# A new fixed order of work in an attention + SiLU kernel: one chain of loads, denominators in four steps, other spacing of idle matmuls

## Chip, cores, metric

One core of a Trainium2 chip. The metric is device microseconds of one execution. A run is marked slow when it is over 1.5% above the fastest of the same kernel; ratios are taken from fast runs alone. Every comparison below is with runs of the kernel before on the same chip.

## The reference

Polynomial-sketch attention (4 batches, 4 heads, 1088 rows, head size 32, sketch size 8), whose output feeds a feed-forward layer with SiLU:

```python
def phi(x):                                    # 8 x 8 products of two sketches
    a = np.einsum('rd,bhsd->bhsr', S1, x)
    b = np.einsum('rd,bhsd->bhsr', S2, x)
    return np.einsum('bhsi,bhsj->bhsij', a, b).reshape(*x.shape[:-1], r * r)
q_p, k_p = (phi(q), phi(k))
kv  = np.einsum('bhsf,bhsd->bhfd', k_p, v)
z   = np.sum(k_p, axis=2)
num = np.einsum('bhsf,bhfd->bhsd', q_p, kv)
den = np.einsum('bhsf,bhf->bhs', q_p, z)[..., None] + 1e-06
x   = (num / den).transpose(0, 2, 1, 3).reshape(4352, 128)
h   = x @ w_in                                 # 128 -> 2048
out = (h / (1 + np.exp(-h))) @ w_out           # 2048 -> 128
```

## The kernel before

The kernel first lists all its work as tasks: an engine (or a choice of two), a cost in us, what it needs. A long constant, ORDER, then says in which order the tasks are issued and, where there is a choice, on which engine. A small model replays that order to choose buffers, and to decide how many idle matmuls to put in front of each TensorE task before the second layer starts. An idle matmul multiplies zeros and nobody reads its result; it is there to keep TensorE busy, so that its clock rises sooner.

```python
ORDER = """
0 7 74 28 23 1 29 24 2.1 22 33 4 3.0 30 25 32 8 34 97 31 35 42.1 11 5 140 40.0 37 6 36 102 55 50 16
...                                            # cut: number of a task, ".1" picks the second engine
"""

def emit(self, text, handles, fill, until):    # in class Plan
    seq = self.order(text)
    self.replay(seq)                           # modelled start and end of each task
    last = 0.0
    for t, c in seq:
        if t["on"] == "PE":
            if last < until():
                fill(last, min(t["start"], until()))
            last = t["end"]
        ...                                    # cut: calls the task's function

def fill(lo, hi):                              # until(): the modelled start of the first h
    step = 0.213 if lo < 4.6 else 0.11
    for _ in range(max(0, int((hi - max(lo, 0.9) - 0.02) / step))):
        nc.tensor.matmul(hold["bank"][:, 0:256], zero[:, 0:P], zero, start=True, stop=True)

def scale():                                   # denominators of a whole batch: one task on VectorE
    nc.vector.tensor_tensor(out=aw[:, :, 0:R], in0=grp(0), in1=grp(2), op=ALU.mult)
    nc.vector.tensor_reduce(out=st["den"], in_=aw, axis=AX.X, op=ALU.add)
    nc.vector.reciprocal(out=st["den"], in_=st["den"])
    nc.vector.tensor_tensor(out=st["aqs"], in0=grp(0), in1=_bc(st["den"], 1, R), op=ALU.mult)

def dmat(i):                                   # qp -> qt by a transposing DMA, on SP's queue
    nc.sync.dma_start_transpose(st["qt", i], st["qp", i].rearrange("p g i j -> p (g i j)"))
```

Names in the profile: PE is TensorE, DVE VectorE, ACT ScalarE, POOL GpSimd, and SP the engine whose queue (SPq) issues most of the DMAs. Kx, Qx, Vf are loaded inputs; KT, QT their 32 x 32 transposes (VectorE); kab and qabm the sketches; kp and qp the products of sketches; KV, kvx, KVd the key-value sums; xT the attention output; H the 2-buffer TensorE result of the first matmul, G its SiLU (ScalarE); ot the final output.

## Time and profile before

| | kernel before |
|---|---|
| time, median of 3 runs | 99.42 us (98.66 to 99.92) |
| span of the profiled run | 97.2 us |
| first SiLU starts | 17.61 |
| batch 1: its keys' first transpose on VectorE | 15.39 |
| batch 1: its first SiLU (number 17 of 68) | 39.32 |
| from there to the end | 57.9 |

These are starts, in us from the span's start. Two rows of the page before, in 40 slices of 2.4 us, matter later: TensorE's busy tenths and the clock that was granted to it.

```profile
PE   5999979969999769999999999999499999999910
PEclk9999999999999999999999999999999999999997
```

The single 4 (near 68 us) is batch 3's numerator, for which TensorE waits. The clock row shows full speed from the start, though the matmuls of the first 10 us run at half rate: this row does not show the warm-up.

### The profile page before, as it was taken

How to read it: one execution, taken by the hardware profiler on the slowest of the kernel's cores; microseconds unless marked ns; L12 is line 12 of the kernel's file. 1: busy time of each engine (PE TensorE's matmuls, PEld its weight loads, DVE VectorE, ACT ScalarE, POOL GpSimd, SP SyncE). 2: the span in 40 equal slices, each digit the busy share in tenths (PEclk: the TensorE clock that was granted, in tenths of full speed). 3: DMA queues.
4: the chain of work that ended last, by engine and by line, in shares of the span. 5: the costliest groups of instructions: out<-in, count | busy, mean ns of one | idle time of the engine just before them, and what ended most of it. 6: DMA issues, size and time to landing. Idle time of an engine off the chain costs nothing.

```text
span 97.2 us, 2474 instructions
## 1 busy us (share of the span) xinstructions
PE 86.4 (89%) x961; PEld 51.4 (53%) x970; DVE 56.7 (58%) x148; ACT 74.0 (76%) x95; POOL 38.3 (39%) x48
## 2 busy tenths in 40 slices
PE   5999979969999769999999999999499999999910
PEld 4545548746677434444533444444244477879900
DVE  5676589999899999999744962804132220022210
ACT  3321546958899929899998799999589999999810
POOL 5048705199998980089920059900000000000000
PEclk9999999999999999999999999999999999999997
DMA  1998999978952573336960000968210336004420
GB/s 34 262 304 226 321 414 402 346 230 253 328 231 61 104 140 59 84 88 133 182 126 4 0 0 8 166 99 152 44 27 0 59 49 108 7 22 85 75 76 14
DMA packets 28506, 12.93 MB, mean 133 GB/s; under 512 B 23120, under 2 KB 26704, under 8 KB 28496
## 3 DMA queue, kind: packets, MB, share of 16 engines
q1 hardware_dynamic: 28256, 12.72, 50.3%
q8 instruction: 7, 0.11, 0.5%
q10 hardware_dynamic: 240, 0.07, 0.3%
q14 instruction: 3, 0.02, 0.1%
HBM read 8.79 MB, written 2.23 MB: 113 GB/s over the span
## 4 chain that ended last, share of the span: by engine, by line
PE 72%; DVE 13%; DMA 5%; SPq 3%; issue 2%; DVEq 0%
PE H L726 25%; PE B L743 21%; PE B L869 7%; PE B L740 6%; DMA qt<-qp 5%; DVE KT L304 3%; SPq L698 3%; PE H L618 2%; PE H L272 2%; PE B L272 2%; DVE qp L646 2%; PE B L333 1%; DVE QT L610 1%; PE B L658 1%; DVE ot L748 1%
## 5 line engine op out<-in xcount | busy, mean ns | idle before, releaser
L730 ACT ACTIVATE G<-H 128x1024 bf16<-128x1024 f32 x68 | 64.8, 1034 | 6.0 <-PE H L726 5.4
L726 PE MATMUL H<-xT,w_in 128*128 128x512 bf16 (+1 forms) x157 | 37.5, 336 | 0.0
L743 PE MATMUL B<-G,w_out 128*128 128x512 bf16 (+1 forms) x122 | 30.9, 351 | 0.6 <-issue 0.3
L726 PEld LDWEIGHTS <-w_in 128*128 128x128 bf16 x176 | 18.4, 114 | 10.8 <-issue 2.2
L327 POOL TENSOR_TENSOR kp<-kab 128x512 bf16<-128x512 f32 (+1 forms) x18 | 17.9, 1014 | 1.9 <-DVE kab L321 1.9
L743 PEld LDWEIGHTS <-w_out 128*128 128x128 bf16 x128 | 12.1, 98 | 10.3 <-issue 0.9
L646 POOL TENSOR_TENSOR qp<-aqs,qabm 128x1024 bf16<-128x1024 f32 (+1 forms) x5 | 10.1, 2019 | 13.7 <-DVE aqs L641 13.7
L869 PE MATMUL B<-zero 128*128 128x256 bf16 x52 | 10.5, 353 | 1.1 <-DVE fmask L233 1.1
L304 DVE STREAM_TRANSPOSE KT<-Kx 128x576 f32<-128x576 f32 (+4 forms) x10 | 9.1, 955 | 0.9 <-DMA Kx<-in_k_dram 0.9
L748 DVE STREAM_TRANSPOSE ot<-B 128x512 f32<-128x512 f32 (+1 forms) x8 | 5.1, 642 | 7.1 <-PE B L743 6.9
L869 PEld LDWEIGHTS <-zero 128*128 128x128 bf16 x52 | 5.9, 122 | 3.6 <-DVE fmask L233 1.0
L164 DVE COPY ot<-B 128x128 f32<-128x128 f32 x5 | 1.3, 287 | 10.3 <-PE B L740 10.3
L478 POOL TENSOR_TENSOR qp<-aqs,qabm 128x512 bf16<-128x512 f32 (+1 forms) x4 | 4.8, 1203 | 6.1 <-DVE aqs L473 6.1
L740 PE MATMUL B<-w_out,G 128*128 128x128 bf16 x96 | 6.7, 219 | 0.0
L740 PEld LDWEIGHTS <-G 128*128 128x128 bf16 x96 | 6.0, 98 | 0.8
L164 DVE CAST xT<-B 128x512 bf16<-128x512 f32 (+1 forms) x6 | 3.7, 636 | 3.7 <-PE B L658 3.7
L646 DVE TENSOR_TENSOR qp<-aqs,qabm 128x1024 bf16<-128x1024 f32 (+1 forms) x4 | 4.4, 1126 | 0.0
L610 DVE STREAM_TRANSPOSE QT<-Qx 128x1024 f32<-128x1024 f32 x3 | 3.6, 1210 | 0.0
L630 DVE STREAM_TRANSPOSE qabm<-H 128x256 f32<-128x256 f32 x6 | 2.5, 417 | 1.9 <-PE B L618 1.9
L618 PE MATMUL H<-QT,WQ 32*32 32x288 f32 x48 | 2.3, 412 | 1.3 <-DVE QT L612 1.3
L499 PE MATMUL B<-identb,qp 128*128 128x128 bf16 x18 | 1.8, 220 | 1.7 <-DVE kab L321 0.9
L327 DVE TENSOR_TENSOR kp<-kab 128x512 bf16<-128x512 f32 x3 | 2.9, 976 | 0.0
(103 smaller groups left out, 78.2 us busy)
## 6 DMA issues: line engine op xcount, KB each, us to landing
Kx<-in_k_dram SPq DMA_DIRECT2D x3, 544.0 KB, 7.0
Qx<-in_q_dram SPq DMA_DIRECT2D x3, 544.0 KB, 6.4
out_dram<-ot SPq DMA_DIRECT2D x24, 64.0 KB, 2.0
Vf<-in_v_dram SPq DMA_DIRECT2D x8, 144.0 KB, 4.1
Vf<-in_v_dram SPq DMA_DIRECT2D x8, 128.0 KB, 3.2
w_inf<-in_moe_w_in_dram SPq DMA_DIRECT2D x2, 512.0 KB, 7.1
w_outf<-in_moe_w_out_dram SPq DMA_DIRECT2D x4, 256.0 KB, 9.4
out_dram<-ot SPq DMA_DIRECT2D x18, 32.0 KB, 1.6
```

The source lines that it names most:

```text
L164: eng.tensor_copy(out=out, in_=in_)
L304: nc.vector.transpose(out=dst, in_=src.rearrange("p c a d -> p c (a d)"))
L327: eng.tensor_tensor(out=st["kp"][:, H * lo: H * hi], in0=_bc(a, 2, R), in1=_bc(bb, 1, R), op=ALU.mult)
L478: eng.tensor_tensor(out=st[f"qp{lo}"], in0=_bc(st["aqs"][:, H * lo: H * hi], 2, R), in1=_bc(bq.rearrange("p a (h r) -> p (a h) r", h=H), 1 ...
L610: nc.vector.transpose(out=QT[:, :, 0: 32 * NB].rearrange("p c (a s) -> p a c s", s=32), in_=Qx[b][:, 0: 4 * NB, :].rearrange("p (a c) d -> ...
L646: eng.tensor_tensor(out=st["qp", i], in0=_bc(st["aqs"][:, g0: g0 + n], 2, R), in1=_bc(grp(1)[:, g0: g0 + n], 1, R), op=ALU.mult)
L726: nc.tensor.matmul(view(sl, i), w_inj[:, (J * jp + i) // 4, (J * jp + i) % 4, :], x, start=True, stop=True)
L730: nc.scalar.activation(out=sl, in_=cc[jp], func=ACT.Silu)
L740: nc.tensor.matmul(d[:, 0:P], view(cc["g", jp], i)[:, P * t: P * (t + 1)], w_out[:, j, :], start=(j == 0), stop=(j == NJ - 1))
L743: nc.tensor.matmul(cc["o"][:, :n], w_out[:, j, :], view(cc["g", jp], i), start=(j == 0), stop=(j == NJ - 1))
L748: nc.vector.transpose(out=cc["ot"][:, :n], in_=cc["o"][:, :n])
L869: nc.tensor.matmul(hold["bank"][:, 0:256], zero[:, 0:P], zero, start=True, stop=True)
```

## The change

Its intent: start the second layer sooner and close the waits inside it. The order was searched again (with noise on the modelled durations), the loads were tied into one chain so that the search could not permute them, each denominator became four tasks so that other work can stand between them, and the idle matmuls got another spacing in the model. The diff, cut:

```diff
 ORDER = """
-0 7 74 28 23 1 29 24 2.1 22 33 4 3.0 30 25 32 8 34 97 31 35 42.1 11 5 140 40.0 37 6 36 102 55 50 16
+0 7 22 28 23 1 29 24 2.1 25 33 3.0 30 80 32 8 34 106 31 35 38.1 11 5 40.0 36 14 37 6 55 16 50 111
 ...                                           # the whole list is new
-    def scaled(b, aq, mq, lo, hi):            # four instructions, one task (scale() likewise)
+    def scale_tasks(b, aq, mq, g0, n, deps, nm):
+        ...
+        for name, cost, fn, tt in (("prod", 0.07 + 0.0084 * n, prod, True), ("red", 0.07 + 0.0095 * n, red, False),
+                                   ("rec", 0.09 + 0.0078 * n, rec, False), ("norm", 0.07 + 0.0084 * n, norm, True)):
+            deps = [pl.add("DVE", cost, fn, deps, lag=0.1, tt=tt, name=nm(name))]
+        return deps[0]
...
-            c = dma(60 * n, dmat, [o], issue=1.3 if n > 1 else 1.2, lag=1.9, name=nm("dmat"))
+            c = dma(60 * n, dmat, [o], issue=1.3 if n > 1 else 1.2, lag=2.1, name=nm("dmat"))
...
+    loads = ["lqa"] + [f"lv0{c}" for c in range(4)] + ["lqb", "lwi0", "lk1", "lwi1", "lwo0", "lwo1", "lq1", "lwo2", "lwo3"]
+    for b in range(1, B):
+        loads += [f"lk{b}"] * (b > 1) + [f"lv{b}{c}" for c in range(4)] + [f"lq{b}"] * (b > 1)
+    for n0, n1 in zip(loads, loads[1:]):
+        named[n1]["deps"].append(named[n0])
...
     def fill(lo, hi):
-        step = 0.213 if lo < 4.6 else 0.11
+        step = 0.213 if lo < 7.0 else 0.15
```

The instructions of the work itself stay the same in kind and number; 52 idle matmuls become 36.

## The prediction

> **What bounds the kernel now.** I read, in this order, the page's busy times and slices, the costliest groups, ACT's timeline, the chain of work, PE's waits, and SP's timeline.
>
> ```profile
> PE 86.4 (89%) x961; PEld 51.4 (53%) x970; DVE 56.7 (58%) x148; ACT 74.0 (76%) x95; POOL 38.3 (39%) x48
> L730 ACT ACTIVATE G<-H 128x1024 bf16<-128x1024 f32 x68 | 64.8, 1034 | 6.0 <-PE H L726 5.4
> L726 PE MATMUL H<-xT,w_in 128*128 128x512 bf16 (+1 forms) x157 | 37.5, 336 | 0.0
> L743 PE MATMUL B<-G,w_out 128*128 128x512 bf16 (+1 forms) x122 | 30.9, 351 | 0.6 <-issue 0.3
> L869 PE MATMUL B<-zero 128*128 128x256 bf16 x52 | 10.5, 353 | 1.1 <-DVE fmask L233 1.1
> ```
>
> The second layer is 68 units: one PE step into H (L726), one SiLU on ACT (L730), one PE step out (L743 or L740). No SiLU can run before a head has made the first attention output. 52 idle matmuls (L869) fill that head.
>
> ```profile
> 17.61 2.85 ACT L730 ACTIVATE G<-H 128x1024 bf16<-128x1024 f32 x3
> 21.58 1.02 ACT L730 ACTIVATE G<-H 128x1024 bf16<-128x1024 f32 x1 [1.13 <-PE H L726]
> 39.32 1.02 ACT L730 ACTIVATE G<-H 128x1024 bf16<-128x1024 f32 x1 [0.25 <-PE H L726]
> 70.60 1.94 ACT L730 ACTIVATE G<-H 128x1024 bf16<-128x1024 f32 x2 [1.27 <-PE H L726]
> 72.70 12.19 ACT L730 ACTIVATE G<-H 128x1024 bf16<-128x1024 f32 x13 [0.16 <-PE H L726]
> 89.12 2.86 ACT L730 ACTIVATE G<-H 128x1024 bf16<-128x1024 f32 x3 [0.24 <-PE H L726]
> ```
>
> The first SiLU starts at 17.61, the last ends at 91.98, and 5.2 us of last products, copies and stores follow. At full pace a SiLU costs (12.19 - 1.03) / 12 = 0.93 us, so 68 need 63.5 us plus about 2 us of other ACT work; 74.4 us passed. PE's floor is higher: steps in steady state start 0.435 us apart (chain pieces of 0.43), so 68 x 2 x 0.435 = 59.2 us. Attention of batches 1 to 3 and the rest of batch 0 adds, from chain and timeline pieces: three each of key projection 0.72, key sum 0.31, its product 0.18, KV 0.44, query projection 0.78 and numerator 0.34, together 8.3, and transposes and small products 2.5. Floor 70 us; from PE's first step at 16.91 to its last at 92.66, 75.7 us passed. So the time is **head, 70 us of PE, PE's stalls (5.7 us), tail**.
>
> ```profile
> 7.40 0.61 PE H L272 x16
> 8.01 0.40 PE B L802
> 8.42 1.28 PE B L869 x6
> 9.70 0.46 PE B L333 x18
> 10.16 0.33 PE B L869
> ```
>
> This is the chain in the head. The key sum (L333) needs DVE's transposes, done at 8.63, but starts at 9.70: six idle matmuls stand in front. An earlier chain piece has eight of them in 1.82 us ahead of the L272 above, whose input was ready at 6.45.
>
> ```profile
> PE B L658 <- DMA qt<-qp: 1.4, 1, 1.4
> PE H L618 <- DVE QT L612: 1.3, 1, 1.3
> PE B L499 <- DVE kab L321: 0.9, 1, 0.9
> 60.95 3.07 SPq L698 DMA_DIRECT2D out_dram<-ot  x6
> 64.56 1.37 SPq L652 DMA_TRANSPOSE qt<-qp  x1
> ```
>
> PE's stalls: batch 3's numerator waits 1.4 us for a transpose that POOL had fed by 61.26 but SP issued at 64.56, behind six stores; batch 2's query projection waits 1.3 us for DVE.
>
> **What the Trainium skill says.** "TensorE: Matmul & The Clock Gate", Part 1: PE runs at half its 2.4 GHz until a window of about 3.4 us has been busy. The trace agrees on the rate: 1.28 / 6 = 213 ns is 256 columns at 1.2 GHz, and the four idle matmuls at 12.25 start 110 ns apart. It does not agree on the time: pieces turn fast only near 10.2 us, after nine busy us. Same page, "Architectural detail": matmuls run strictly in order, VectorE and ScalarE are strict FIFO. The trace agrees: during the 1.4 us wait on L658, ACT ran dry for 1.27. "SBUF — State Buffer", "SBUF: two separate sides": VectorE with two SBUF inputs and GpSimd lock each other out. The trace agrees: a 1024-column qp on DVE takes 1.22 us at 41.59, and two take 2.79 beside a POOL qp at 30.18. "DMA: Bandwidth & Descriptors", "Issuing engines are not separate DMA queues": transfers interleave. The trace agrees: the w_in loads took 5.8 and 8.3 us, with other loads in flight.
>
> **The change, part by part.**
>
> *Idle matmuls.* The static orders show 36 in place of 52. Between the key projections four stand where eight stood; before the key sum two where six stood. I rework the head with the durations above. Second key projection: PE is free at 5.58 + 4 x 0.23 = 6.5, DVE's KT ends at 6.45, start 6.6 (was 7.40). L802 ends at 7.6, two idle ones at 8.05, the transposes at 7.85: key sum at 8.05 (was 9.70). Then zt, query projection, L349 and WM follow as before, slower by some tenths because PE may be cold: the projection with WM at about 10.4 (was 11.96), the first denominator product at 11.1 (was 12.79). Its four steps take 1.1 us, here with one transpose and one other product between (0.35): the first qp at 12.45 (was 13.88). From that start the old path took 3.73 us to the first SiLU (17.61), and nearly the same pieces stand on it. **Head: -1.4 us.**
>
> *Separate denominator steps.* The four instructions per group remain (0.23 to 0.49 us each on DVE); nothing is saved in work. Others now go between: about neutral, and for batches 0 and 2 it lets a transpose that PE waits for go first.
>
> *Order of work for batch 1.* In the old order DVE does batch 2's key transposes (L304, 1.05 + 0.96) and a second qp of batch 1 (1.4) ahead of things that PE needs. Now the key transposes come after batch 1's first qp, and the second goes to POOL beside it. By hand, DVE's queue gives: batch 0's last group 18.7, batch 1's query transpose 21.4, its projection back by 24.6, denominators 26.8, qp 28.2, POOL's qp 29.5, second transpose issued by 31, numerator at 34.8. The old numerator stood at 37.03. But DVE now has a wait of its own: kvx and KVd of batch 1 come only behind batch 2's key and query transposes, at about 34.1, and the copy of xT behind another 1.05. I get the first SiLU of batch 1 at about 37.0 (was 39.32): **2.3 us ahead, so 0.9 beyond the head**; the PE order has done two more output steps by then (+0.9) and one query projection less (-0.8), which cancel.
>
> *Stores and loads.* Batch 3's three transposes now stand together on SP with no store between, and its two large qp run on DVE and POOL at once (old: 4.25 us in a row on POOL). By the same count they are issued by 60 and land by 64; PE reaches that numerator behind SiLU 49, at about 67. **-1.4 us** if it holds. Loading k2 after w_out and q1 takes one load out of the crowd at 7 to 20 us; the old head shows only 0.84 us of ACT waiting on it, off the chain: 0.
>
> *Given back.* Each query projection takes one of the two H buffers until DVE has emptied it (the old trace shows a 1.01 us ACT gap at 53.98), and that remains. At 16 to 18 us PE meets a key projection whose DVE input I place at 17.4, 0.9 us after PE is ready: already in my 37.0. Later misfits of a new order: +0.6, my guess.
>
> Sum: -1.4 - 0.9 - 1.4 + 0.6 = -3.1. PE's floor checks it: from about 15.5, 70 us and 3.6 of stalls end at 89.1; plus 4.5 of tail is a span of 93.6, -3.6. I take -3.6 to -3.7 and add it to the median: 99.4 - 3.7 = **95.7 us**.
>
> **The rivals.** *Cold clock.* 16 fewer idle matmuls leave PE less busy, so the doubling could come one window (3.4 us) later, near 13.6, or PE could fall back before the first SiLU. For it: the old kernel needed nine dense us. Against: the pieces removed were cold ones in front of real work. It would cost 0.2 to 0.3 us on each of some four pieces on the path and 0.4 per early step: 97 to 98 us.
> *A new DVE wait eats the gain.* kvx of batch 1 sits behind 3 us of transposes; if keys of batch 2 or 3 land late, that grows and PE's in-order queue stops. For: it is the worst wait in my count, and DVE is dense from 21 to 48. Against: loads come earlier. Near 97.5.
> *PE is full anyway.* Slices from 72 on show 9, so an earlier attention may only pile up output steps. That leaves head and numerator: 96.5 to 97.
> *Upside.* If the order also removes the H-buffer gap and the 0.15 to 0.25 us gaps, 93.5.
>
> **Range and chances.** The head gain is the firmest (one visible queue); the other two lean on a count by hand with perhaps 1.5 us of error. I predict 95.7, range 93.4 to 98.0. The limit for faster is 97.4, about one error above my centre: faster 0.80, same 0.17, slower 0.03.
>
> **What would show it.** Right: 36 idle matmuls, none between the end of DVE's kab and the key sum for more than 0.3 us; first SiLU at 15.9 to 16.5; first SiLU of batch 1 at 36 to 38; no DMA wait at the numerator of batch 3; ACT gaps over 0.5 us summing to under 4; tail 5 us as before. Wrong: idle matmuls at 213 ns beyond 11 us, or first steps of 256 columns 0.21 us apart (cold); a wait of PE on kvx or QT over 2 us around 31 to 37; transposes still landing after PE asks.

## The result

The changed kernel took **96.29 us** (median of 4 runs, 95.87 to 96.43) beside 99.19 us of the kernel before (4 runs, 98.66 to 99.92). The ratio of the fast runs is **0.9696**, 95% interval 0.9623 to 0.9769. A ratio here is the mean time of one kernel's fast runs over the mean of the other's in the same rounds, so it is not quite the ratio of the quoted medians.

The page after, the lines that answer to those in the prediction (busy us, share of the span, count):

```profile
PE 84.7 (90%) x943; PEld 48.7 (52%) x954; DVE 57.2 (61%) x151; ACT 73.1 (78%) x92; POOL 37.0 (39%) x48
L733 ACT ACTIVATE G<-H 128x1024 bf16<-128x1024 f32 x68 | 64.5, 1043 | 6.3 <-PE H L729 5.2
L879 PE MATMUL B<-zero 128*128 128x256 bf16 x36 | 8.0, 355 | 1.1 <-DVE fmask L234 1.1
```

The SiLU work is what it was (64.5 us); ScalarE's idle time in front of it has even grown by 0.3 us. The span shrank because the same row of SiLUs starts sooner and its largest late gap is gone. ScalarE's timeline after (start, length, line, group, count, idle before):

```profile
16.45 1.94 ACT L733 ACTIVATE G<-H 128x1024 bf16<-128x1024 f32 x2
37.78 1.02 ACT L733 ACTIVATE G<-H 128x1024 bf16<-128x1024 f32 x1 [0.98 <-PE H L729]
39.54 8.61 ACT L733 ACTIVATE G<-H 128x1024 bf16<-128x1024 f32 x9 [0.74 <-PE H L729]
54.75 6.72 ACT L733 ACTIVATE G<-H 128x1024 bf16<-128x1024 f32 x7 [1.01 <-PE H L729]
61.68 12.17 ACT L733 ACTIVATE G<-H 128x1024 bf16<-128x1024 f32 x13 [0.20 <-PE H L729]
```

The first SiLU starts at 16.45 (before: 17.61), the first of batch 1 at 37.78 (39.32). SiLU 49, which began at 72.70 before, is the tenth of the last group: 61.68 + 9 x 0.93 = 70.05. There is no gap of 1.3 us near it any more. The gap of 1.01 at the query projection of batch 2 is still there.

Why the late gap went, in SP's timeline after: four transposes, batch 3's three among them, stand together ahead of the stores.

```profile
58.84 6.19 SPq L655 DMA_TRANSPOSE qt<-qp  x4
65.13 12.00 SPq L701 DMA_DIRECT2D out_dram<-ot  x12
```

And what TensorE waits for now (total, times, longest, in us), four of the list's six lines; the other two are 1.1 us before the first idle matmul and 0.3 us of "issue". No DMA is in the list:

```profile
PE B L273 <- DVE KT L305: 1.4, 2, 0.8
PE B L513 <- DVE qp L495: 1.2, 2, 0.8
PE B L513 <- POOL qp L495: 0.7, 1, 0.7
PE B L394 <- DVE kvx L165: 0.3, 1, 0.3
```

Two of these lie later: 0.5 us of the first line at 31.6, for batch 2's keys, and the wait on kvx. The rest is in the head or just behind it. The chain of work that ended last shows what is new: it now runs through the load of batch 1's keys and then along VectorE's queue.

```profile
7.15 7.59 DMA Kx<-in_k_dram
14.76 1.10 DVE KT L305
16.74 1.12 DVE KT L305
17.97 0.60 DVE aqs L485
18.60 0.99 DVE qp L495
```

The 7.59 us from issue to landing were off the chain before. A head that is done sooner meets a load that is not.

**The span in parts.** With "k1" for the start of batch 1's key transposes and "17" for the first SiLU of batch 1:

| profiled run | first SiLU | k1 | 17 | span | k1 to 17 | 17 to end |
|---|---|---|---|---|---|---|
| before | 17.61 | 15.39 | 39.32 | 97.2 | 23.9 | 57.9 |
| after | 16.45 | 14.76 | 37.78 | 94.2 | 23.0 | 56.4 |

0.6 us come from an earlier k1, 0.9 from a shorter way to batch 1's first SiLU, 1.5 from what follows: 3.0 us together, the difference of the spans. These are two single executions. In a second profile of the changed kernel (experiment 4) the three parts were 0.9, 1.5 and 1.4.

### The profile page after: what moved, and what is told of

It is laid out like the page before. It is cut to its first block, busy times and chain, and to the rows that moved or that the text cites. A ratio compares the mean times of both kernels' runs of the same rounds, so it can differ in the third digit from the quotient of the medians.

```text
span 94.2 us, 2445 instructions
## 1 busy us (share of the span) xinstructions
PE 84.7 (90%) x943; PEld 48.7 (52%) x954; DVE 57.2 (61%) x151; ACT 73.1 (78%) x92; POOL 37.0 (39%) x48
## 4 chain that ended last, share of the span: by engine, by line
PE 60%; DVE 20%; DMA 11%; SPq 3%; issue 2%; DVEq 0%
PE H L729 26%; PE B L746 20%; DMA Kx<-in_k_dram 11%; DVE KT L305 8%; PE B L743 6%; SPq L191 2%; PE H L630 2%; DVE qabm L640 2%; DVE qp L649 1%; DVE aqs L485 1%; DVE QT L622 1%; DVE qp L495 1%; DVE den L479 1%; DVE AW L476 1%; PE B L384 1%
## 5 line engine op out<-in xcount | busy, mean ns | idle before, releaser
L733 ACT ACTIVATE G<-H 128x1024 bf16<-128x1024 f32 x68 | 64.5, 1043 | 6.3 <-PE H L729 5.2
L729 PE MATMUL H<-xT,w_in 128*128 128x512 bf16 (+1 forms) x151 | 36.3, 335 | 0.0
L746 PE MATMUL B<-G,w_out 128*128 128x512 bf16 (+1 forms) x126 | 31.9, 352 | 0.6 <-issue 0.3
L328 POOL TENSOR_TENSOR kp<-kab 128x512 bf16<-128x512 f32 (+1 forms) x18 | 18.3, 1039 | 11.1 <-DVE kab L322 11.1
L649 POOL TENSOR_TENSOR qp<-aqs,qabm 128x1024 bf16<-128x1024 f32 (+1 forms) x4 | 7.2, 1808 | 9.7 <-DVE aqs L485 9.7
L305 DVE STREAM_TRANSPOSE KT<-Kx 128x512 f32<-128x512 f32 (+4 forms) x10 | 9.3, 953 | 1.7 <-DMA Kx<-in_k_dram 1.7
L879 PE MATMUL B<-zero 128*128 128x256 bf16 x36 | 8.0, 355 | 1.1 <-DVE fmask L234 1.1
L649 DVE TENSOR_TENSOR qp<-aqs,qabm 128x1024 bf16<-128x1024 f32 (+1 forms) x5 | 6.9, 1405 | 0.1
L879 PEld LDWEIGHTS <-zero 128*128 128x128 bf16 x36 | 4.0, 124 | 2.8 <-DVE fmask L234 1.1
L165 POOL CAST w_in<-w_inf 128x512 bf16<-128x512 f32 x3 | 1.9, 641 | 4.5 <-DMA w_inf<-in_moe_w_in_dram 4.5
L495 POOL TENSOR_TENSOR qp<-aqs,qabm 128x512 bf16<-128x512 f32 (+1 forms) x3 | 3.6, 1214 | 0.0
L165 POOL CAST Vh<-Vf 128x1152 bf16<-128x1152 f32 x3 | 3.4, 1143 | 0.0
```

The source lines that it names most:

```text
L165: eng.tensor_copy(out=out, in_=in_)
L305: nc.vector.transpose(out=dst, in_=src.rearrange("p c a d -> p c (a d)"))
L328: eng.tensor_tensor(out=st["kp"][:, H * lo: H * hi], in0=_bc(a, 2, R), in1=_bc(bb, 1, R), op=ALU.mult)
L495: eng.tensor_tensor(out=st[f"qp{lo}"], in0=_bc(st["aqs"][:, H * lo: H * hi], 2, R), in1=_bc(bq.rearrange("p a (h r) -> p (a h) r", h=H), 1 ...
L649: eng.tensor_tensor(out=st["qp", i], in0=_bc(st["aqs"][:, g0: g0 + n], 2, R), in1=_bc(grp(1)[:, g0: g0 + n], 1, R), op=ALU.mult)
L729: nc.tensor.matmul(view(sl, i), w_inj[:, (J * jp + i) // 4, (J * jp + i) % 4, :], x, start=True, stop=True)
```

## Experiments

Twelve kernels ran, in three groups; all gave correct results, each with six runs (one with five) beside eleven of the kernel before (medians 99.34, 99.24 and 99.56). Task names in the diffs stand for the numbers in ORDER: k1kt00 is a transpose of batch 1's keys, lk1 its load, lwo0 a load of w_out, q3dmat0 a transposing DMA of batch 3, m10st1 a store. "Frozen" means that the idle matmuls were put at fixed places, so that the edit could not change them through the model.

### 1. The idle matmuls alone (kernel before)

```diff
-        step = 0.213 if lo < 4.6 else 0.11
+        step = 0.213 if lo < 7.0 else 0.15
```

> The kernel before with the new spacing of the idle matmuls alone (38 in place of 52), order untouched. Theory (idle matmuls at the cold clock stood in front of the key projection and the key sum): the key sum starts near 8.1 us in place of 9.7, the first SiLU near 16.5 in place of 17.6, and 0.5 to 1.1 us of that reaches the end: ratio 0.989 to 0.995. Rival 1 (the head was shortened by the new order on DVE and ACT, not by the idle matmuls): first SiLU within 0.3 us of 17.6, ratio 0.998 to 1.002. Rival 2 (fewer idle matmuls leave PE cold): first steps of 256 columns 0.21 us apart, ratio over 1.0.

Measured: 99.39 us, ratio **0.9983** (0.9942 to 1.0023): no gain that can be measured, though the interval leaves room for 0.6%. The head did move: the key sum started at 8.23 in place of 9.63, and the first SiLU at 16.91 in place of 17.61. Not all of that is the spacing: in two other profiled runs with the old spacing (experiments 2 and 8) the key sum started at 9.37 and 7.80 and the first SiLU at 17.08 and 17.16, since the moment at which the matmuls turn fast differs between executions (last section). VectorE's and ScalarE's timelines say what ate the gain:

```profile
15.22 2.18 DVE L304 STREAM_TRANSPOSE KT<-Kx 128x576 f32<-128x576 f32 x2 [1.15 <-DMA Kx<-in_k_dram]
13.85 0.63 ACT L162 ACTIVATE w_in<-w_inf 128x512 bf16<-128x512 f32 x1 [1.93 <-DMA w_inf<-in_moe_w_in_dram]
21.40 1.02 ACT L730 ACTIVATE G<-H 128x1024 bf16<-128x1024 f32 x1 [1.25 <-PE H L726]
```

VectorE reached batch 1's key transposes 1.15 us before the keys had landed, so k1 came only 0.17 us sooner than before, and ScalarE waited 1.93 us for w_in. The fourth SiLU, 21.58 before, came at 21.40, and everything behind it is 0.2 us early. The run of experiment 8 in the old order shows the same bound: its key sum came at 7.80, yet VectorE then waited 1.80 us for batch 1's keys, and k1 stood at 15.37, where it had been. The theory that half or more of the head's gain reaches the end is not borne out: the measured ratio lies outside the expected 0.989 to 0.995, of which the interval still holds a part.

### 2. One transposing DMA ahead of the stores (kernel before)

```diff
-... q3dmat1 m10st1 m14st0 m10st0 q3dmat0 m14st1 ...
+... q3dmat1 q3dmat0 m10st1 m14st0 m10st0 m14st1 ...
```

> The kernel before with one transpose of batch 3 issued ahead of the stores of batch 1 on SP in place of behind six of them. Theory: the 1.4 us wait of PE at batch 3's numerator goes away and PE, the bound from there on, ends 1.0 to 1.4 us earlier: ratio 0.986 to 0.990. Rival (PE has a backlog of output steps, or the stores now hold something else up): the wait goes but the end moves by under 0.3 us, ratio 0.997 to 1.0.

Measured: 98.04 us, ratio **0.9885** (0.9836 to 0.9934), so 1.15% or 1.1 us. The wait of 1.4 us at batch 3's numerator is gone (0.3 us of waiting for a transposing DMA remain at its last rows), and ScalarE's timeline has one run of SiLUs where it had a gap of 1.27:

```profile
63.73 19.78 ACT L730 ACTIVATE G<-H 128x1024 bf16<-128x1024 f32 x21 [0.23 <-PE H L726]
```

"17 to end" is 56.7 us instead of 57.9. The theory held: moving one issue is worth about a third of the whole change.

### 3. Both (kernel before)

> The kernel before with the new spacing of the idle matmuls and with batch 3's first transpose issued ahead of the stores, nothing else. If the two parts add as measured alone (0.9983 and 0.9885): 0.987. Theory: what the head gains alone is swallowed at batch 1 by the key load and the order of work, so the pair stays at 0.984 to 0.990, well above the whole change (0.966), and the missing 2 per cent need the new order with its loads. Rival: the 1.5 us wait at batch 3's numerator hid the head's gain; then the pair gives 0.980 or less.

Measured: 97.84 us, ratio **0.9843** (0.9804 to 0.9882), where the product of the two is 0.9868. The two add, within the intervals; "17" at 38.87, "17 to end" 56.3. So about half of the 3.4% that the next experiment finds for the whole change (0.9659) is not in these two parts.

### 4. The changed kernel again, and with the old spacing of idle matmuls

```diff
-        step = 0.213 if lo < 7.0 else 0.15
+        step = 0.213 if lo < 4.6 else 0.11
```

> The changed kernel itself, as the yardstick of this chip: ratio 0.970 (0.962 to 0.977 measured before).

> The changed kernel with the old spacing of the idle matmuls (47 in place of 36), order untouched. Theory: the first SiLU comes 0.9 to 1.2 us later, about 17.5. But in the changed kernel DVE waits 0.9 us at 14.8 for the load of batch 1's keys, and the chain that ends last runs through that load, so only 0.2 to 0.6 us should reach the end: ratio 0.972 to 0.977. Rival (the head carries to the end in full): 1.0 us or more, ratio 0.980 or over.

Measured: the changed kernel 96.09 us, ratio **0.9659** (0.9615 to 0.9703); with the old spacing (47 idle matmuls in this order) 96.81 us, ratio **0.9740** (0.9694 to 0.9786). Inside the new order the spacing is worth 0.8%, and the ratio lies in the expected range; inside the old order it was worth 0.2%. The intervals of these two differences overlap, so that the new order makes it worth more is likely and not shown. In the profiled runs k1 moved from 15.76 to 14.46 and "17" from 38.61 to 36.94; with the old spacing VectorE found the keys landed, with the new one it waited 0.15 us. "17 to end" is 56.5 in both. (These profiles are of the fastest run of the one kernel and one of the slower runs of the other, 95.54 and 97.22 us; the effect is the 0.7 us between the medians, not the 1.7 between the two "17".)

### 5. No idle matmul at all (changed kernel)

```diff
-        for _ in range(max(0, int((hi - max(lo, 0.9) - 0.02) / step))):
+        for _ in range(0):
```

> The changed kernel without any idle matmul. Theory: they only buy the clock; without them PE's head pieces run at half rate (256 columns in 213 ns) until PE is dense, past 17 us, and the first SiLU comes 1 to 2 us later: ratio 0.975 to 0.990. Rival: the head's own matmuls warm the clock soon enough, and the pieces in front of which nothing now stands start sooner: 0.962 to 0.970.

Measured: 96.29 us, ratio **0.9721** (0.9665 to 0.9778), between the two expectations. TensorE's timeline shows the half rate up to 17.9 us: the first eight steps of 256 columns take 1.63 us where they took 1.04 with idle matmuls.

```profile
15.77 0.63 PE L513 MATMUL B<-identb,qp 128*128 128x128 bf16 x4
16.45 1.63 PE L729 MATMUL H<-xT,w_in 128*128 128x256 bf16 x8
```

The first SiLU came at 17.49, 1.0 us later than after the change. Yet "17" came at 37.55, no later than after the change (37.78). So, as far as single profiles show, the idle matmuls do buy the clock, and the clock does buy the first SiLU, but most of that is waiting time further on. Four profiled runs with the changed kernel's order in the head say the same: where the matmuls turned fast at about 4.7 us (experiment 4), 9.2 (the first profile), 13.8 (kvx moved, experiment 8) and 17.9 (here), the first SiLU came at 16.17, 16.45, 16.77 and 17.49, but the spans were 93.4, 94.2, 93.7 and 94.0. How much of the time they buy is between nothing and about 1%; the intervals don't say more.

### 6. Denominator steps contiguous again (changed kernel, frozen)

```diff
-... q0prod0_0 k0kv3 q0backm20 k0outer6 lk2 q0red0_0 ... q0norm0_0 ... q0prod2_0 q0outer00 ...
+... q0backm20 q0prod0_0 k0kv3 k0outer6 lk2 q0red0_0 ... q0norm0_0 ... q0outer00 q0prod2_0 ...
 # likewise k1kt00 ahead of q0prod4_4 and k3tr10 behind q2norm
```

> The changed kernel with the four denominator steps of each group in a row again, nothing woven in (three places: batch 0 twice, batch 2 once), all other orders and the idle matmuls as in the changed kernel. Prediction's step: neutral, ratio within 0.002 of the changed kernel (0.964 to 0.968). Rival (weaving hides the latency between dependent DVE steps, some 0.1 us each, or lets a needed transpose go first): 0.3 us or more slower, ratio 0.969 or above.

Measured: 96.06 us, ratio **0.9671** (0.9617 to 0.9725), "17" at 37.12, span 93.6. Neutral: weaving other work between the four steps gains nothing that can be measured; the intervals leave room for about 0.7% either way.

### 7. The order of the loads (changed kernel, frozen)

```diff
# a_k1first
-loads: ... lqb lwi0 lk1 lwi1 lwo0 lwo1 lq1 lwo2 lwo3 ...
+loads: ... lqb lk1 lwi0 lwi1 lwo0 lwo1 lq1 lwo2 lwo3 ...
# a_k2early
+loads: ... lqb lwi0 lk1 lwi1 lwo0 lwo1 lk2 lq1 lwo2 lwo3 ...
# a_oldloads: the loads as in the kernel before, up to batch 2's values
+loads: lqa lqb lv01 lv02 lv00 lv03 lwi0 lk1 lwi1 lk2 lq1 lwo1 lwo2 lwo0 ...
```

> The changed kernel with batch 1's key load issued ahead of the first half of w_in; the idle matmuls frozen at the 36 of the changed kernel. New theory (what is left of the head is bounded by the landing of batch 1's key load, 14.7 us in the changed kernel's trace, where DVE waits 0.9 us): the keys land at 14.0 or earlier, the third SiLU starts 0.4 us or more earlier, ratio to the kernel before 0.959 to 0.964 (changed kernel on the last chip 0.966). Rival (that landing is only one of several inputs that come at the same time; w_in comes later and holds up its casts on POOL and ACT): first SiLU later by 0.3 us or more, ratio 0.966 or above.

> The changed kernel with one load moved: the keys of batch 2 go ahead of the queries of batch 1, right behind the second w_out piece (there the old kernel had them before all w_out pieces). Idle matmuls frozen. Theory (w_out piece 0 third in line was what hurt with all of the old load order, by the casts that wait for it in order): batch 1's keys land as before within 0.3 us, and the time stays within 0.5 per cent of the changed kernel: 0.966 to 0.972. Rival (one more large load in the crowd slows all the others): batch 1's keys and the w_in pieces land 0.5 us or more later, and the time is 1 per cent or more up: 0.976 and over.

> The changed kernel with the loads in the old order up to the last v load of batch 2 (second half of queries 0 ahead of values 0, keys 2 and queries 1 ahead of w_out, values 1 and 2 mixed), idle matmuls frozen. The prediction's step (load order is worth nothing): ratio within 0.002 of the changed kernel, 0.964 to 0.968. New theory (batch 1's keys share the engines with more loads and land later, near 15.2): 0.4 to 0.8 us slower, ratio 0.970 to 0.975.

Measured, batch 1's keys first: ratio **0.9695** (0.9629 to 0.9762), with three of six runs slow. k1 came at 14.03 without a wait, but the w_in casts came later (GpSimd waited 4.04 us for w_in, and TensorE then 1.9 us for a qp of GpSimd, which stands behind that cast), the first SiLU at 17.79, "17" at 37.56: no gain. The keys are one of several inputs that arrive at about the same time.

Measured, batch 2's keys early: ratio **0.9666** (0.9606 to 0.9725), no loss. (This rests on three fast runs of six; its profiled run was slow, so when the keys and w_in landed in a fast run is not known.)

Measured, the loads in the old order: 99.22 us, ratio **0.9971** (0.9909 to 1.0032): nearly the whole gain was gone. The profiled run was a slow one (granted clock 0.972), so its sums are not compared; but one wait, for a transfer and not for an engine, is plain in GpSimd's timeline and in the waits:

```profile
21.88 0.62 POOL L164 CAST w_out<-w_outf 128x512 bf16<-128x512 f32 x1 [4.04 <-DMA w_outf<-in_moe_w_out_dram]
PE B L745 <- POOL w_out L164: 2.2, 1, 2.2
PE B L512 <- POOL qp L494: 1.4, 1, 1.4
```

```profile
17.78 0.61 POOL L165 CAST w_out<-w_outf 128x512 bf16<-128x512 f32 x1
```

The second fence is the same cast in the changed kernel: at 17.78, without a wait. The new order casts w_out's piece 0 first, on GpSimd, ahead of a qp; the old loads bring piece 0 as the third of four. GpSimd's queue stops, the qp behind the cast comes late, and TensorE stops twice. As batch 2's keys alone did no harm, the place of the w_out pieces is the likely cause; it is not shown, since the places of the queries' and values' loads were changed as well (TensorE also waited 0.9 us for a cast of batch 0's values) and were not tried alone. The converse (new loads under the old order) was not run: there VectorE transposes batch 2's keys at 19.06, and the new loads bring them only behind 18 others, so such a kernel would show nothing but that wait.

### 8. Order of work for batch 1

In the kernel before (52 idle matmuls, frozen):

```diff
-... k1kt20 ... k2kt00 k1tr10 ... k2kt20 ... k2proj ... k2tr00 k2tr10 k2z k2zt k2l2 ... q1outer0 ... q1outer1 (VectorE) ...
+... k1kt20 ... k1tr10 ... q1outer0 k2kt00 k2kt20 ... q1outer1 (GpSimd) ... m04h4 k2proj ... k2tr10 k2tr00 ... k2z k2zt k2l2 k2wm q2proj ...
```

> The kernel before, with its loads and its 52 idle matmuls (frozen) as they are, and only the order of work for batch 1 taken from the changed kernel: batch 2's key transposes, key projection, key sum and WM go behind batch 1's first qp, and the second qp of batch 1 goes from DVE to POOL. Theory (my prediction's third step): DVE reaches batch 1's qp 2 to 3 us sooner, the first SiLU of batch 1 comes 0.5 to 1 us sooner than 39.3, and the end 0.4 to 0.9 us sooner: ratio 0.991 to 0.996. Rival: the first SiLU of batch 1 is held by another queue (POOL's second qp beside DVE, or kvx behind batch 2's transposes), and nothing is gained or something is lost: 0.997 to 1.01.

In the changed kernel (frozen): kvx and KVd of batch 1 ahead of an output's transpose and of batch 3's keys, and batch 1's numerator ahead of batch 2's l2 product:

```diff
-... k3kt20 k1kv k2outer6 ... m02tr k2z k1kvm ... k1kvc k3kt00 k2l2 ... q1num ... k2wm ...
+... k3kt20 k1kv k1kvm m02tr k2outer6 ... k2z ... k1kvc ... q1num k2l2 ... k2wm k3kt00 ...
```

> The changed kernel with batch 1's kvx copy ahead of an output transpose, batch 3's second key transpose moved behind the xT copy into a stretch where DVE waits, and batch 1's numerator ahead of a small product on PE; idle matmuls frozen. Theory (the wait that the new order made: kvx, KVd and xT of batch 1 behind key transposes on DVE, predicted as a rival): first SiLU of batch 1 0.5 to 0.9 us earlier, ratio 0.957 to 0.962. Rival (PE is full from there, or the query projection of batch 2 just waits in its place): under 0.2 us, ratio 0.964 to 0.968.

Measured, in the kernel before: 100.46 us, ratio **1.0117** (1.0081 to 1.0154), so slower. "k1 to 17" grew from 23.9 to 25.2 us, "17 to end" stayed 57.9. The edit did what it was meant to on VectorE: batch 1's first qp began at 29.10 (before 30.18), and VectorE was done with its part at 30.3 (before 32.97); GpSimd ended the second at 32.1. But TensorE's order still had batch 2's query projection (L617) ahead of batch 1's numerator (L657), and that projection needs batch 2's keys, which now came later:

```profile
36.01 0.43 PE L617 MATMUL H<-QT,WQ 32*32 32x288 f32 x2 [0.36 <-DVE WQ L163]
...
38.17 0.41 PE L657 MATMUL B<-qt,KVd 64*32 64x512 bf16 x8
```

The projection began at 36.01 in place of 34.80, and the numerator at 38.17 in place of 36.96, both 1.2 us later. What VectorE won, TensorE's queue lost. In the changed kernel the numerator (35.69) stands ahead of that projection (37.67); my edit had left this out. So this run tests less than the step it was meant for, and shows that half of such a reordering can cost more than none.

Measured, in the changed kernel: 95.84 us, ratio **0.9658** (0.9608 to 0.9708). TensorE's wait on kvx was gone, "k1 to 17" was 22.2 us (22.5 in the changed kernel of experiment 4), and the time was the same. The wait on kvx that my rival feared costs nothing here that can be measured. No variant that ran is faster than the changed kernel beyond the intervals.

## Why the prediction was right

The time came out 0.6 us above the predicted 95.7, inside the range and on the likely side. Of the signs that it named for being right, one was missed: ScalarE's gaps over 0.5 us sum to 4.2 us (before: 5.2), not to under 4. By its own steps:

**Head, -1.4 us: the mechanism was right, the size too large.** 36 idle matmuls, the key sum at 7.94 (I had 8.05), the first SiLU at 16.45 (I had 15.9 to 16.5): 1.16 us sooner. But the sum took all of it to the end. Shown: with the idle matmuls alone 0.2% reaches the end, and 0.8% inside the new order; in the profiles k1 came 0.63 us sooner, and 0.93 in experiment 4's. The term should have been about 0.6 to 0.9. (One of its sums slips as well: 11.1 + 1.1 + 0.35 is 12.55, not 12.45, so its own terms give 1.3.) What I had missed is the sentence about the loads: I saw "0.84 us of ACT waiting" and called it "off the chain: 0". It was off the chain only as long as the head was slow. A transfer that lands just in time is the next bound, and its place is seen by comparing landing time and first use, not by looking for a wait.

**Separate denominator steps, "about neutral": right**, experiment 6.

**Order for batch 1, -0.9 beyond the head: right in size, not shown in its cause.** "k1 to 17" fell from 23.9 to 23.0, and it is 22.9 with the old spacing in the new order. I put it down to batch 2's key transposes leaving VectorE's way. That move alone, without the order on TensorE that belongs to it, lost 1.2%. Which of the many moves between 15 and 38 us make up the 0.9 stays open; they come as a set. My count also had batch 1's numerator at 34.8 and "17" at 37.0, where they came at 35.69 and 37.78: 0.8 to 0.9 us early, which is the size of the wait for batch 1's keys (0.87 us) that it had not foreseen. In the profile of experiment 4, where that wait was 0.15 us, "17" came at 36.94.

**Batch 3's transposes, -1.4 us: right.** "17 to end" fell by 1.5; the one-line edit alone gave 1.1 us and 1.2 in that part of its profile.

**Load order, 0: wrong as it stood.** With the loads in the old order, the new order of work loses 3.1% (0.9971 against 0.9659). It is no gain by itself, but a condition. The likely reason is that casts stand in fixed queues, so that the load which such a queue asks for first must come first.

**Given back, +0.6: did not happen.** "17 to end" is 56.4 to 56.5 us in every fast profiled run of the new order, whatever "17" was. This cancelled most of the error in the head: 0.6 + 0.9 + 1.5 - 0 = 3.0 against the 3.1 of my sum. The median moved by 3.1 (99.42 to 96.29; 2.9 from the 99.19 of the same rounds), not by the 3.7 that I had subtracted in the end after checking with TensorE's floor. That check assumed 3.6 us of stalls without deriving them: from TensorE's first step at 15.82 to its last, which ends at 90.18, 74.4 us passed, not 73.6. That the plain sum, 3.1, fits so well is in part luck, since the error in the head and the 0.6 that was not given back cancel.

**The rivals.** Of "a new DVE wait eats the gain", a wait of VectorE appeared, but for batch 1's keys and not on kvx, and in that run it took about half of the head's term. "PE is full anyway" fell: the numerator and the head did not add up to the result (0.9843 against 0.9659). "Cold clock" was looked at in the wrong way. I tied it to the number of idle matmuls. The profiled runs show that the moment at which the matmuls turn fast differs between executions of the same head, as the next section shows, and in experiment 5, where it came over 8 us late, it cost at most about 1%.

One place for the reader of the prediction: that matmuls stay in order is said in Part 2 of the page that it cites; the section that it names says it of VectorE and ScalarE, and of TensorE's queue that it can pull weight loads ahead.

## What to carry to other kernels

Before you shorten a stage, write down when each of the next stage's inputs lands: a transfer without a wait today is the bound of tomorrow, and the gain ends there. In a kernel of in-order queues, a reordering is a set of moves over all engines and the loads; take one out and it can cost nearly all that the whole gained (here the loads, 3.1 of 3.4%), or make a part slower than nothing (1.2%), so test moves alone but judge them together. A single transfer that is issued behind others on one queue while something needs it is the exception: it can be moved alone, and here it was about a third of the gain.

## What the Trainium skill lacked or had wrong

- "TensorE: Matmul & The Clock Gate", Part 1, says that the transition comes after about 4 us of sustained work, varying by 500 ns from run to run with the phase of a free-running window of about 3.4 us. (It also calls the number of slow matmuls variable, 6, 11 or 14 in one kernel, and warns that the throttle has been seen stuck for over 50 us.) Here it varied by over 9 us between executions whose first 4.3 us on TensorE are the same: the changed kernel's pieces turned fast at about 4.7 us in one run, about 9.2 in another, and near 13.8 in a third, all with 36 idle matmuls in the same places. TensorE's timeline in the head: first the changed kernel's run in experiment 4, then its first profiled run, then that with kvx moved (experiment 8), whose head is the same. In the first, 16 matmuls of 160 columns took 0.50 us where the second took 0.79; at 9.5 the second ran five idle matmuls in 0.71 where the third took 1.25. The head had short gaps and waits; that only a window without them counts is a guess that no run tests.

```profile
4.74 0.50 PE L273 MATMUL H<-KT,WP 64*32 64x160 f32 x16
```

```profile
4.80 0.79 PE L273 MATMUL H<-KT,WP 64*32 64x160 f32 x16
9.48 0.71 PE L879 MATMUL B<-zero 128*128 128x256 bf16 x5
```

```profile
9.78 1.25 PE L879 MATMUL B<-zero 128*128 128x256 bf16 x5
14.07 0.60 PE L879 MATMUL B<-zero 128*128 128x256 bf16 x4
```

- The same part says nothing of what idle matmuls cost in front of real work in an in-order queue, or whether they pay; it only puts the whole warm-up under 1% of a typical kernel's span. Here: 14 fewer gained 0.2% in the old order, within the noise, and 11 fewer 0.8% in the new; none at all left the half rate until 17.9 us and cost between nothing and about 1%.
- No page I used says that the row of the granted clock in a profile page doesn't show this warm-up (the same part only warns that a trace's throttle events can be unreliable): it reads full speed in slices where 256 columns take 213 ns.
- "DMA: Bandwidth & Descriptors", "Issuing engines are not separate DMA queues", says that transfers share the engines and interleave, which the runs agree with (7.59 us from issue to landing for batch 1's keys). What it lacks is the consequence for order: putting those keys ahead of w_in let VectorE start on them 0.43 us sooner (k1 at 14.03 against 14.46, now without a wait), made the casts of w_in later, and gained nothing (0.9695 against 0.9659), while the old order of all the loads cost 3.1%.
